# Inverse powers of one head pair and half of a decayed tile on GpSimd, row numbers at a later item, and loads of 96 rows in place of 128

## The chip, the cores and the metric

The kernel runs on one core of a Trainium2 chip. The metric is the device time of one execution in microseconds (us), taken as the median of several runs of the same program. Engine names are those of the profile: PE is TensorE (matmuls), PEld its weight loads, DVE is VectorE, ACT is ScalarE, POOL is GpSimd and SP is SyncE, which here only issues DMAs.

## The reference

Two blocks follow each other. The first is a linear recurrence over time (RWKV): 4 batches, 8 heads, 768 steps, head dimension 48.

```
for t in range(S):
    cur     = (u * k[t]) outer v[t]
    y[t]    = r[t] @ (state + cur)
    state   = w[:, None] * state + k[t] outer v[t]
```

The outputs are laid side by side as x (4 x 768 x 384) and go through a gated mixture of 8 experts: a token takes the expert with the largest logit, or, where a locality gate says so, the expert of the token before it; the result is p[e] * relu(x w1[e]) w2[e], with 1024 hidden units.

## The kernel before

**Items.** The attention is worked through in 16 items. Item n is batch n // 4 and head pair hp = n % 4; two heads of 48 rows lie in partitions 0 to 47 and 64 to 111, and the 16 rows behind each are zeros. The 768 steps are cut into 6 chunks of 128. Within a chunk the decay is taken out by scaling: r times powers of w (`rw`), k times inverse powers of w (`kw`), so that the chunk's inner part is an ordinary masked matmul; between chunks a state is carried.

**Per item, by engine.** POOL makes `pd` = r k (L217), `ke` = k times the powers up to the chunk's end (L213), and from item 3 on `rw` (L230, through `decayed`). DVE makes `kw` (L237), for items 0 to 2 also `rw` (L230), masks the scores into `am` (L293), multiplies `y` by v (L276) and scans the states `S` (L255). PE does the scores (L291, in two halves), the own term (L268), `added` (L249, k v products), `inside` (L300), `before` (L313) and the transposes of a finished item (L332). ACT copies results out of PSUM.

**Order.** The code's order is the order of each engine; `run` writes it out by hand. In iteration n an item's scores and own term are made, then `added`, `states`, and `scale(n + 1)`, which is POOL's work for the next item. `inside`, `before` follow in the next iteration. The early iterations 0, 1 and 2 have an order of their own.

**Powers of w.** `tab` in SBUF holds, for each head pair, powers 0 to 128 of w and of a reciprocal of w. `reciprocals(i)` refines the inverse powers by one Newton step: two DVE instructions (L156, L157) of which the second writes `inv[:, i]` into PSUM, where `kw` reads it. `self.first` is a copy in PSUM of the powers of the pair that is being worked on, made by ACT (L377, L392); it shares the bank `mp` with `T`, where `added` puts its sums. `reciprocals(0)` runs at the start, 1 in iteration 0, 2 in iteration 1 and 3 in iteration 3.

**Loads.** `load(n)` issues three DMAs on SP's queue: `rk` (r and k, 768 KB), `kv` (k and v by tokens, 584 KB) and `vT` (v transposed, 384 KB); `rk` of item 0 goes in two halves. Items 0 to 2 are loaded ahead of the loop, item n + 3 at the top of iteration n. `rk` and `vT` have `AHEAD` = 4 buffers, `kv` has 5, so that item n writes over item n - 4 (n - 5 for `kv`). SP's queue is worked through in order, and a DMA that waits for its buffer holds up those behind it.

**Router.** `numbering` makes nine tables of whole numbers with POOL's iota (L636), in iteration 2 ahead of `scale(3)`; `cast` has ACT turn six of them into floats in iteration 6 (L690). Their first reader is `experts_of(0, (0,))` in iteration 9. The experts' matmuls (L1134 and after) begin when the attention is done.

**Banks.** `banks` hands out two pairs of PSUM banks in turn; `warm(n)` takes the next pair and issues n transposes of the identity into it (L163), whose result is not used. In iteration 0 `warm(3)` stands between `turn_ends` (L173, L174: the turned powers of pairs 1 to 3, `endT`) and `added(0)`.

Of the kernel before, what the change touches and what calls it, by code (L numbers as in the profile page):

```python
# [11 lines left out]
F32 = mybir.dt.float32  # L12
I32 = mybir.dt.int32
Act = mybir.ActivationFunctionType
Alu = mybir.AluOpType
# [5 lines left out]
P = 128  # L21
B, H, S, DH = 4, 8, 768, 48
HP = H // 2
DP = 64
# [4 lines left out]
NCH = S // P  # L29
# [32 lines left out]
class Attention:  # L62
# [13 lines left out]
    def __init__(self, tc, st, rk_d, kv_d, vT_d, x_d, w_t, wp_d, kept, ident, lt, mp):  # L76
        self.tc, self.nc = tc, tc.nc
        nc = tc.nc
        self.rk_d, self.kv_d, self.vT_d, self.x_d = rk_d, kv_d, vT_d, x_d
        self.w_t, self.kept, self.ident, self.lt = w_t, kept, ident, lt  # L80

        self.late = st.enter_context(tc.tile_pool(name="late", bufs=1))
        self.wp = self.late.tile([P, H, 32], F32, name="wp")
        self.inner = ExitStack()

        def pool(name, bufs, **kw):
            return self.inner.enter_context(tc.tile_pool(name=name, bufs=bufs, **kw))

        once = pool("once", 1)
        self.two = pool("two", 2)  # L90
        self.four = pool("four", 4)
        self.py = pool("py", 1, space=PSUM)
        ps = pool("ps", 1, space=PSUM)

        self.pairs = [ps.tile([P, 2, 512], F32, name=f"pair{i}") for i in range(2)]

        self.T = mp[:, 2 * P + 2:2 * P + 2 + (NCH - 1) * DH].rearrange("p (e c) -> p e c", c=NCH - 1)

        self.inv = pool("pinv", 1, space=PSUM).tile([P, HP, P], F32, name="inv")


        n = B * HP - 1
        self.rks, self.vTs = [None] * AHEAD, [None] * AHEAD
        for i in range(1, AHEAD + 1):
            self.rks[(n + i) % AHEAD] = once.tile([P, 2, NCH, P], F32, name=f"rk{i}")
        for i in range(1, AHEAD + 1):
            self.vTs[(n + i) % AHEAD] = once.tile([P, 2, C2, P], F32, name=f"vT{i}")
        self.kvs = [once.tile([P, 2 * VB + DP - DH], F32, name=f"kv{i}") for i in range(AHEAD + 1)]
        self.items = [dict() for _ in range(B * HP)]
        self.xTs, self.xs, self.lTs = {}, {}, {}  # L110
        for i in range(AHEAD - 1):
            self.load(i)
        nc.sync.dma_start(out=self.wp, in_=wp_d)


        self.step = once.tile([P, HP, DH, NCH - 1], F32, name="step")
        nc.vector.memset(self.step, 0.0)


        self.tab = tab = once.tile([P, HP, 2, P + 1], F32, name="tab")  # L120
        nc.vector.memset(tab[:, 0, :, 0:1], 1.0)
        nc.gpsimd.memset(tab[:, 1:, :, 0:1], 1.0)
        w = once.tile([P, HP, 2], F32, name="w")
        nc.vector.tensor_scalar(w[:, :, 0], w_t[:, :, 0], W_LO, W_HI, Alu.max, Alu.min)
        nc.vector.reciprocal(w[:, :, 1], w[:, :, 0])
        nc.vector.tensor_copy(tab[:, 0, :, 1], w[:, 0])
        nc.gpsimd.tensor_copy(tab[:, 1:, :, 1], w[:, 1:])
        n = 2
        while n <= P:
            m = min(n - 1, P + 1 - n)  # L130
            for engine, t in ((nc.vector, tab[:, :1]), (nc.gpsimd, tab[:, 1:])):
                engine.tensor_mul(t[..., n:n + m], t[..., 1:1 + m], t[..., n - 1:n].to_broadcast([P, t.shape[1], 2, m]))
            n += m

        self.first, self.newton = mp[:, :P + 1], mp[:, P + 1:2 * P + 1]
        nc.scalar.copy(self.first, tab[:, 0, 0])
        self.reciprocals(0)

        self.end = once.tile([P, HP, P + DP], F32, name="end")
        self.endT = once.tile([P, 2, HP, 2 * DH], F32, name="endT")  # L140
        self.align(26)
        self.warm(8)
        self.ends(slice(0, 1))
        self.turn_ends(slice(0, 1))
        self.warm(5)
# [7 lines left out]
    def reciprocals(self, i):  # L153

        nc, inv = self.nc, self.tab[:, i, 1, 1:]
        nc.vector.scalar_tensor_tensor(self.newton, self.first[:, 1:], -1.0, inv, Alu.mult, Alu.mult)  # L156
        nc.vector.scalar_tensor_tensor(self.inv[:, i], self.newton, 2.0, inv, Alu.add, Alu.mult)  # L157

    def warm(self, n):

# [28 lines left out]
    def load(self, n):  # L189
        nc = self.nc  # L190
        b, hp = divmod(n, HP)
        rk, vT, kv = self.rks[n % AHEAD], self.vTs[n % AHEAD], self.kvs[n % (AHEAD + 1)]
        if n:
            nc.sync.dma_start(out=rk.rearrange("p a c t -> p (a c t)"), in_=self.rk_d[b, hp])
        else:
            for z in (slice(0, C2), slice(C2, NCH)):
                nc.sync.dma_start(out=rk[:, :, z], in_=self.rk_d[b, hp].rearrange("p (a c t) -> p a c t", a=2, c=NCH)[:, :, z])
        nc.sync.dma_start(out=kv, in_=self.kv_d[b, hp])
        nc.sync.dma_start(out=vT.rearrange("p a c t -> p (a c t)"), in_=self.vT_d[b, hp])
        self.items[n].update(b=b, hp=hp, rT=rk[:, 0], kT=rk[:, 1], vT=vT,  # L200
                             k=kv[:, :VB].rearrange("p (c x) -> p c x", c=NCH), v=kv[:, VB:])

    def scale(self, n):

        nc, t = self.nc, self.items[n]
        t["ke"] = self.two.tile([P, NCH, 2 * DH], F32, name="ke")
        t["pd"] = self.two.tile([P, NCH, P], F32, name="pd")
        t["rw"] = self.four.tile([P, NCH, P], F32, name="rw")
        hp = t["hp"]

        def ke(p):
            z = slice(p, NCH if n == 0 else NCH - 1, 2)
            nc.gpsimd.tensor_mul(t["ke"][:, z], t["k"][:, z], spread(self.endT[:, p, hp], 1, len(range(NCH)[z])))  # L213

        def pd(i):
            z = slice(i * C2, (i + 1) * C2)
            nc.gpsimd.tensor_mul(t["pd"][:, z], t["rT"][:, z], t["kT"][:, z])  # L217

        def rw(i):
            self.decayed(nc.gpsimd, n, slice(i * C2, (i + 1) * C2))  # L220


        for what in (pd, ke) if n < 3 else (ke, rw, pd) if n == 4 else (rw, ke, pd):
            for i in range(2):
                what(i)

    def decayed(self, engine, n, z):
        t = self.items[n]
        pw = self.first[:, :P] if n < 3 else self.tab[:, t["hp"], 0, :P]
        engine.tensor_mul(t["rw"][:, z], t["rT"][:, z], spread(pw, 1, z.stop - z.start))  # L230

    def keys(self, n):
        nc, t = self.nc, self.items[n]
        t["kw"] = self.two.tile([P, NCH, P], F32, name="kw")
        inv = self.inv[:, t["hp"]]
        for z in (slice(0, NCH),) if n > 2 else (slice(0, C2), slice(C2, NCH)):
            nc.vector.tensor_mul(t["kw"][:, z], t["kT"][:, z], spread(inv, 1, z.stop - z.start))  # L237
            if n < 3:
                self.decayed(nc.vector, n, z)

    def added(self, n):
# [113 lines left out]
    def run(self, router, fetch, heads):  # L355
# [11 lines left out]
        for n in range(M + 1):  # L367
            if n + AHEAD - 1 < M:
                self.load(n + AHEAD - 1)
            if n == 0:  # L370
                self.scale(0)
                self.keys(0)
                self.tables()
                self.scores(0, 0)()
                self.scores(0, 1)()
                self.own(0)
                self.nc.scalar.copy(self.first, self.tab[:, 1, 0])  # L377
                self.turn_ends(slice(1, HP))
                self.warm(3)
                self.added(0)  # L380
                self.reciprocals(1)
                self.states(0)
                self.scale(1)
                continue
            if n < 3:

                self.keys(n)
                self.inside(n - 1)
                self.before(n - 1)
                if n == 2:  # L390
                    self.turn(0, pair("tp"))
                self.nc.scalar.copy(self.first, self.tab[:, n + 1, 0])  # L392
                self.scores(n, 0)()
                keep = self.scores(n, 1)
                keep()
                self.own(n)
                self.added(n)
                self.states(n)
                if n == 1:
                    self.reciprocals(2)  # L400
                else:
                    router.numbering()
                self.scale(n + 1)
                continue
            if n < M:
# [19 lines left out]
                router.slots(0)  # L425
            if n == M:
                router.shares(0)
            if n + 1 < M:
                self.scale(n + 1)
            if n == g + 6:  # L430
# [9 lines left out]
                router.same(0, 1)  # L440
            if M - 2 <= n < M:
                fetch(2 * (n - M + 2) + 1)
            if n == 6:
                router.cast()
            if n == M:
                break
# [1331 lines left out]
```

## Time and profile before

| | us |
|---|---|
| median of 3 runs (lowest, highest) | 377.44 (376.11, 377.89) |
| the profiled execution, its own time | 379.17 |
| span from its first to its last instruction | 377.5 |
| PE busy in the span | 363.0 |
| DVE busy | 247.7 |
| POOL busy | 148.7 |
| ACT busy | 110.3 |
| first matmul of the experts (L1134) starts at | 113.02 |

Times in the text are counted from the span's first instruction. The attention is the first 113 us of it, the experts the rest. In the engines' timelines a row gives the start, the time that the group took, the engine, the line, the operation, the tiles written and read, and in brackets how long the engine had been idle and what ended that. A group joins instructions of one line that follow each other.

### The profile page before, as it was taken

How to read it: one execution, taken by the hardware profiler on the slowest of the kernel's cores; microseconds unless marked ns; L12 is line 12 of the kernel's file. 1: busy time of each engine (PE TensorE's matmuls, PEld its weight loads, DVE VectorE, ACT ScalarE, POOL GpSimd, SP SyncE). 2: the span in 40 equal slices, each digit the busy share in tenths (PEclk: the TensorE clock that was granted, in tenths of full speed). 3: DMA queues.
4: the chain of work that ended last, by engine and by line, in shares of the span. 5: the costliest groups of instructions: out<-in, count | busy, mean ns of one | idle time of the engine just before them, and what ended most of it. 6: DMA issues, size and time to landing. Idle time of an engine off the chain costs nothing. (4 is left out here: it accounts for less than half of the span.)

```text
span 377.5 us, 9676 instructions
## 1 busy us (share of the span) xinstructions
PE 363.0 (96%) x3844; PEld 319.6 (85%) x3844; DVE 247.7 (66%) x718; ACT 110.3 (29%) x304; POOL 148.7 (39%) x207
## 2 busy tenths in 40 slices
PE   7899999999989999999999999999999999999992
PEld 6676777786769998999899999999999998989971
DVE  6988778888834835787557656857767767555300
ACT  4132233233532211322332233333243233331210
POOL 7689999786222055212333113313233023021012
PEclk9999999999999999999999999999999999999998
DMA  7999999983669457713352452164165065162011
GB/s 245 417 411 410 407 405 338 370 300 109 196 232 340 160 188 296 299 27 115 140 198 62 147 214 87 49 218 190 38 207 213 22 215 206 21 257 112 2 41 38
DMA packets 17765, 74.93 MB, mean 199 GB/s; under 512 B 2778, under 2 KB 6624, under 8 KB 15408
## 3 DMA queue, kind: packets, MB, share of 16 engines
q1 hardware_dynamic: 10336, 56.89, 40.7%
q0 software_dynamic: 3424, 9.48, 7.4%
q10 hardware_dynamic: 3952, 7.87, 5.7%
q8 instruction: 32, 0.52, 0.6%
q14 instruction: 21, 0.17, 0.1%
HBM read 64.79 MB, written 9.47 MB: 197 GB/s over the span
## 5 line engine op out<-in xcount | busy, mean ns | idle before, releaser
L1333 POOL DMA_INDIRECT out_dram<-yo,sid x27 | 26.6, 985 | 115.5 <-ACT yo L1328 92.0
L1184 PE MATMUL h<-exT,w1t 128*128 128x168 f32 (+4 forms) x240 | 54.9, 327 | 0.0
L1188 DVE TENSOR_TENSOR hT<-h,hs 128x168 f32<-128x168 f32 (+3 forms) x60 | 21.1, 351 | 46.1 <-PE h L1184 29.6
L1107 POOL DMA_INDIRECT xg<-x_d,gid x29 | 31.1, 1072 | 34.1 <-DVE gid L877 15.1
L1184 PEld LDWEIGHTS h<-exT,w1t 128*128 128x128 f32 x240 | 41.6, 190 | 0.3 <-issue 0.3
L1134 PE MATMUL h<-exT,w1t 128*128 128x168 f32 (+2 forms) x192 | 37.2, 333 | 0.5 <-DVE lt L698 0.5
L1253 PE MATMUL y<-factors,sums 128*128 128x192 f32 x168 | 36.8, 326 | 0.0
L293 DVE TENSOR_TENSOR am<-pair,kept 128x768 f32<-128x768 f32 x32 | 30.0, 953 | 8.9 <-PE pair L291 8.4
L217 POOL TENSOR_TENSOR pd<-rk 128x384 f32<-128x384 f32 x32 | 31.5, 1006 | 10.6 <-PE y L268 10.0
L1184 PE MATMUL h<-xs,ws 128*128 128x168 f32 (+4 forms) x144 | 35.3, 327 | 0.0
L1134 PEld LDWEIGHTS h<-exT,w1t 128*128 128x128 f32 x192 | 30.9, 190 | 2.6 <-DVE lt L698 0.6
L1184 PEld LDWEIGHTS h<-xs,ws 128*128 128x128 f32 x144 | 25.5, 190 | 4.3 <-ACT hs L1191 1.2
L1253 PEld LDWEIGHTS y<-factors,sums 128*128 128x128 f32 x168 | 28.9, 190 | 0.2
L291 PE MATMUL pair<-rw,kw 48*64 48x128 f32 (+1 forms) x768 | 23.4, 249 | 1.9 <-issue 1.1
L300 PE MATMUL y<-am,kv 128*64 128x128 f32 x360 | 22.9, 276 | 1.3 <-DVE y L276 1.2
L230 POOL TENSOR_TENSOR rw<-rk,tab 128x384 f32<-128x384 f32 x26 | 23.7, 936 | 0.4 <-DMA rk<-in_rk_dram 0.4
L1121 DVE COPY exT<-tp 128x384 f32<-128x384 f32 (+5 forms) x29 | 13.9, 485 | 14.7 <-PE tp L1120 14.6
L291 PEld LDWEIGHTS pair<-rw,kw 48*64 48x64 f32 x768 | 19.6, 133 | 4.6 <-issue 2.8
L1253 PE MATMUL y<-w2t,hT 128*128 128x192 f32 x96 | 23.0, 328 | 0.0
L213 POOL TENSOR_TENSOR ke<-kv,endT 128x288 f32<-128x288 f32 (+1 forms) x32 | 21.9, 705 | 1.9 <-DMA kv<-in_kv_dram 1.0
L321 ACT COPY xT<-y 128x768 f32<-128x768 f32 x15 | 12.0, 800 | 33.1 <-PE y L313 31.1
L300 PEld LDWEIGHTS y<-am,kv 128*64 128x64 f32 x360 | 19.4, 137 | 2.4 <-DVE y L276 1.7
(298 smaller groups left out, 736.6 us busy)
## 6 DMA issues: line engine op xcount, KB each, us to landing
w1t<-in_w_dram SPq DMA_DIRECT2D x8, 1536.0 KB, 6.9
w2t<-in_w_dram SPq DMA_DIRECT2D x8, 1536.0 KB
rk<-in_rk_dram SPq DMA_DIRECT2D x15, 768.0 KB, 8.4
kv<-in_kv_dram SPq DMA_DIRECT2D x16, 584.0 KB, 7.1
vT<-in_vT_dram SPq DMA_DIRECT2D x16, 384.0 KB
x_d<-x ACTq DMA_DIRECT2D x4, 1152.0 KB
w1t<-in_w_dram SPq DMA_DIRECT2D x2, 768.0 KB
w2t<-in_w_dram SPq DMA_DIRECT2D x2, 768.0 KB
```

Of the source, the lines that this page charges most:

```text
L213: nc.gpsimd.tensor_mul(t["ke"][:, z], t["k"][:, z], spread(self.endT[:, p, hp], 1, len(range(NCH)[z])))
L217: nc.gpsimd.tensor_mul(t["pd"][:, z], t["rT"][:, z], t["kT"][:, z])
L230: engine.tensor_mul(t["rw"][:, z], t["rT"][:, z], spread(pw, 1, z.stop - z.start))
L291: nc.tensor.matmul(sc[f * DP:(f + 1) * DP, h, i, x:], lhsT=t["kw"][q, c, o * DP:(o + 1) * DP], rhs=t["rw"][q, c, x:], start=True, stop=True)
L293: return lambda: nc.vector.tensor_mul(t["am"][:, g], sc, spread(self.kept[:, g:g + 3], 1, 2))
L300: nc.tensor.matmul(t["y"][h][p * DP:(p + 1) * DP, c2 * P:(c2 + 1) * P], lhsT=t["v"][:, (2 * c + h) * DH:(2 * c + h) * DH + DP], rhs=t["am" ...
L1107: self.nc.gpsimd.indirect_dma_start(out=xg[:n], out_offset=None, in_=self.x_d[:rows], in_offset=bass.IndirectOffsetOnAxis(ap=u["gid"][:n, ...
L1134: nc.tensor.matmul(h[:, :n], lhsT=u["w1"][:, m, kk, :], rhs=u["xT"][:, kk, :], start=(kk == 0), stop=(kk == DK - 1))
L1184: nc.tensor.matmul(out, lhsT=a, rhs=b, start=start and k == 0, stop=stop and k == len(terms) - 1, skip_group_check=True)
L1188: nc.vector.tensor_tensor(out, a, b, op=Alu.add)
L1253: return lambda: nc.tensor.matmul(bank[:, x * half:(x + 1) * half], lhsT=a, rhs=b, start=(j == 0 and x == 0), stop=(j == FK // 2 - 1), ski ...
L1333: self.nc.gpsimd.indirect_dma_start(out=out.rearrange("n (h d) -> (n h) d", h=2) if half else out, out_offset=bass.IndirectOffsetOnAxis(ap ...
```

## The change

- `inverse(1)`, three POOL instructions into a new SBUF tile `more` and an ACT copy into `inv[:, 1]`, stands in the place of the two DVE instructions of `reciprocals(1)`. It comes behind `turn_ends` in iteration 0, and `warm(3)` there is gone.
- Of item 2's four `rw`/`kw` pieces on DVE, the second half of `rw` goes to POOL, as the first thing of `scale(2)`; POOL reads the powers from `tab` and not from `self.first`.
- `numbering` and `cast` go from iterations 2 and 6 to iteration 8.
- Items 4 to 15 load partitions 0 to 47 and 64 to 111 of `rk` and `vT`, each in two DMAs of 48 rows; the zeros in the other rows are those that items 0 to 3 left in the four buffers. `kv` stays whole. For item 4 `kv` is issued ahead of `rk`.

```diff
+        self.more = once.tile([P, P], F32, name="more")
...
+    def inverse(self, i):
+
+        nc, w, inv = self.nc, self.tab[:, i, 0, 1:], self.tab[:, i, 1, 1:]
+        nc.gpsimd.tensor_mul(self.more, w, inv)
+        nc.gpsimd.tensor_scalar(self.more, self.more, -1.0, 2.0, Alu.mult, Alu.add)
+        nc.gpsimd.tensor_mul(self.more, self.more, inv)
+        nc.scalar.copy(self.inv[:, i], self.more)
...
-        if n:
-            nc.sync.dma_start(out=rk.rearrange("p a c t -> p (a c t)"), in_=self.rk_d[b, hp])
-        else:
-            for z in (slice(0, C2), slice(C2, NCH)):
-                nc.sync.dma_start(out=rk[:, :, z], in_=self.rk_d[b, hp].rearrange("p (a c t) -> p a c t", a=2, c=NCH)[:, :, z])
-        nc.sync.dma_start(out=kv, in_=self.kv_d[b, hp])
-        nc.sync.dma_start(out=vT.rearrange("p a c t -> p (a c t)"), in_=self.vT_d[b, hp])
+        rows = (slice(0, P),) if n < AHEAD else (slice(0, DH), slice(DP, DP + DH))
+        src = self.rk_d[b, hp].rearrange("p (a c t) -> p a c t", a=2, c=NCH)
+        if n == AHEAD:
+            nc.sync.dma_start(out=kv, in_=self.kv_d[b, hp])
+        for z in (slice(0, NCH),) if n else (slice(0, C2), slice(C2, NCH)):
+            for q in rows:
+                nc.sync.dma_start(out=rk[q, :, z], in_=src[q, :, z])
+        if n != AHEAD:
+            nc.sync.dma_start(out=kv, in_=self.kv_d[b, hp])
+        for q in rows:
+            nc.sync.dma_start(out=vT[q].rearrange("p a c t -> p (a c t)"), in_=self.vT_d[b, hp][q])
...
+        if n == 2:
+            rw(1)
         for what in (pd, ke) if n < 3 else (ke, rw, pd) if n == 4 else (rw, ke, pd):
...
     def decayed(self, engine, n, z):
-        pw = self.first[:, :P] if n < 3 else self.tab[:, t["hp"], 0, :P]
+        pw = self.first[:, :P] if n < 3 and engine is self.nc.vector else self.tab[:, t["hp"], 0, :P]
...
     def keys(self, n):
-            if n < 3:
+            if n < 2 or n == 2 and z.start == 0:
                 self.decayed(nc.vector, n, z)
...
                 self.turn_ends(slice(1, HP))
-                self.warm(3)
+                self.inverse(1)
                 self.added(0)
-                self.reciprocals(1)
                 self.states(0)
...
                 if n == 1:
                     self.reciprocals(2)
-                else:
-                    router.numbering()
...
+            if n == HP * 2:
+                router.numbering()
             if n + 1 < M:
                 self.scale(n + 1)
...
-            if n == 6:
+            if n == HP * 2:
                 router.cast()
```

## The prediction

> **What bounds the kernel now.** The chain that ended last holds nothing here but the final scatter, so I read the stretches first (columns: PE, PEld, DVE, ACT, POOL busy with counts, granted clock, share of the DMA engines, GB/s).
>
> ```profile
> 28.00:45.00 17.00, 15.99 (x373) 11.57 (x362) 13.26 (x35) 3.50 (x8) 17.00 (x21) 1.00 1.02 410
> 45.00:104.00 59.00, 58.11 (x1270) 44.61 (x1270) 48.99 (x76) 20.16 (x53) 43.76 (x52) 1.00 0.80 291
> ```
>
> From 45 us on PE has no idle time worth the name; between 28 and 45 PE, POOL and the DMA engines are all nearly full, so the order of waiting must tell which one leads. The change's first two parts lie ahead of that, in items 0 to 2. There I read DVE's and PEld's timelines against each other.
>
> ```profile
> 10.64 0.96 DVE L276 TENSOR_TENSOR y<-y,vT 128x768 f32<-128x768 f32 x1
> 12.22 0.30 DVE L156 SCALAR_TENSOR_TENSOR mp<-mp,tab 128x128 f32<-128x128 f32 x1 [0.63 <-PE mp L249]
> ...
> 12.77 0.64 DVE L255 TENSOR_TENSOR_SCAN S<-step,mp 128x240 f32<-128x240 f32 x1
> 13.32 0.53 DVE L237 TENSOR_TENSOR kw<-rk,inv 128x384 f32<-128x384 f32 x1
> ...
> 14.70 0.55 DVE L230 TENSOR_TENSOR rw<-rk,mp 128x384 f32<-128x384 f32 x1
> 15.37 1.82 DVE L293 TENSOR_TENSOR am<-pair,kept 128x768 f32<-128x768 f32 x2
> 17.11 0.96 DVE L276 TENSOR_TENSOR y<-y,vT 128x768 f32<-128x768 f32 x1
> ...
> 21.99 1.89 DVE L293 TENSOR_TENSOR am<-pair,kept 128x768 f32<-128x768 f32 x2 [0.72 <-PE pair L291]
> ```
>
> ```profile
> 10.78 0.34 PEld L163 LDWEIGHTS pair<-ident 128*128 128x128 f32 x3
> 11.29 0.66 PEld L249 LDWEIGHTS mp<-kv,ke 128*64 128x64 f32 x20 [0.17 <-issue]
> 11.87 1.29 PEld L300 LDWEIGHTS y<-am,kv 128*64 128x64 f32 x24
> 13.46 0.68 PEld L313 LDWEIGHTS y<-rw,S 48*48 48x48 f32 x20 [0.30 <-DVE S L255]
> 14.43 0.57 PEld L291 LDWEIGHTS pair<-rw,kw 48*64 48x64 f32 x24 [0.29 <-issue]
> 15.30 0.54 PEld L291 LDWEIGHTS pair<-rw,kw 48*64 48x64 f32 x24 [0.30 <-DVE rw L230]
> ...
> 18.12 1.29 PEld L300 LDWEIGHTS y<-am,kv 128*64 128x64 f32 x24 [0.95 <-DVE y L276]
> 19.58 0.68 PEld L313 LDWEIGHTS y<-rw,S 48*48 48x48 f32 x20 [0.17 <-issue]
> 20.41 0.58 PEld L332 LDWEIGHTS pair<-ident,xT 112*128 112x128 f32 x6
> 21.14 0.54 PEld L291 LDWEIGHTS pair<-rw,kw 48*64 48x64 f32 x24
> ```
>
> In iteration 1 DVE leads: PE waits for `S`, for `rw`, then 0.95 us for `y`. In iteration 2 it is turned round: DVE has done `rw` and waits 0.72 us for PE's scores, which start when the transposes are through. So what DVE is spared in iteration 1 counts, and what it is spared in iteration 2 need not. POOL's rows and SP's (each SP issue here waits until the transfer eight issues before it has landed) give the third limit:
>
> ```profile
> 8.93 1.56 POOL L213 TENSOR_TENSOR ke<-kv,endT 128x288 f32<-128x288 f32 x2
> ...
> 13.88 1.36 POOL L213 TENSOR_TENSOR ke<-kv,endT 128x288 f32<-128x288 f32 x2 [1.03 <-DMA kv<-in_kv_dram]
> 16.77 1.96 POOL L217 TENSOR_TENSOR pd<-rk 128x384 f32<-128x384 f32 x2 [1.53 <-PE y L268]
> ...
> 20.00 0.15 POOL L636 IOTA ie_i<- 128x8 int32 x1
> ...
> 20.83 0.13 POOL L636 IOTA ief_i<- 1x8 int32 x1
> 21.37 1.69 POOL L230 TENSOR_TENSOR rw<-rk,tab 128x384 f32<-128x384 f32 x2 [0.42 <-DMA rk<-in_rk_dram]
> ...
> 27.19 1.35 POOL L213 TENSOR_TENSOR ke<-kv,endT 128x288 f32<-128x288 f32 x2 [0.89 <-PE y L313]
> ...
> 56.22 1.97 POOL L217 TENSOR_TENSOR pd<-rk 128x384 f32<-128x384 f32 x2 [0.55 <-PE y L268]
> ```
>
> ```profile
> 21.36 0.33 SPq L199 DMA_DIRECT2D vT<-in_vT_dram  x1
> 22.81 0.33 SPq L194 DMA_DIRECT2D rk<-in_rk_dram  x1
> 23.77 0.33 SPq L198 DMA_DIRECT2D kv<-in_kv_dram  x1
> ...
> 27.10 0.33 SPq L194 DMA_DIRECT2D rk<-in_rk_dram  x1
> ```
>
> Eight issues back, these four stand for the landings of `rk`, `kv`, `vT` of item 3 and `kv` of item 4. POOL's starts at 21.37 and 27.19 are thus landings (the profile names PE at 27.19, but the matmul that frees that buffer was long done; the `pd` at 16.77 I take for `rk` of item 2 in the same way). Loads hold POOL up until 27.19 and not after.
>
> **The change, part by part.**
>
> *`warm(3)` gone.* Three transposes, 0.34 us of weight loads, and the 0.17 us idle behind them: `added(0)` can begin at about 10.85 and not 11.29, 0.44 us sooner; its `ke` was done at 8.93 + 1.56 = 10.49. `inside(0)` gains less, since it needs `y`: 10.64 + 0.96 = 11.60, and 0.05 us on (as at 18.12, behind 17.11 + 0.96) is 11.65 in place of 11.87. As heaters the transposes are not missed: PE waits longer, 0.95 us, at 18.12, and the granted clock after it is 1.00. The pairs of banks change places from here on; the only one in use, that of `endT`, is read by 11.71 (below): 0.
>
> *`reciprocals(1)` gone from DVE.* L156 waited for `added(0)` to end; now the scan stands there, at 12.22 - 0.44 = 11.78 in place of 12.77, and `kw`, `rw` follow 0.99 us sooner: the first `kw` at 12.33, the last `rw` done at 14.70 + 0.55 - 0.99 = 14.26. PE takes over as the limit: L313 starts 1.46 us behind L300 (19.58 - 18.12), at 13.11; the scores 0.83 us after that (20.41 - 19.58), at 13.94, with the first half's `rw` there, and the second half's before it is wanted; `am` 0.85 us on (21.99 - 21.14), at 14.79, against 15.37. **Gain 0.58 us.** `y` of item 1 moves by the same, 17.11 to 16.53.
>
> *`inverse(1)` on POOL and ACT.* The nearest rows, with mean ns of one after the bar:
>
> ```profile
> L132 POOL TENSOR_TENSOR tab<-tab 128x192 f32<-128x192 f32 x1 | 0.5, 512 | 0.1
> L132 POOL TENSOR_TENSOR tab<-tab 128x96 f32<-128x96 f32 x1 | 0.4, 352 | 0.1
> masks.py:199 POOL TENSOR_SCALAR_AFFINE_SELECT ident<-ident 128x128 f32<-128x128 f32 x1 | 0.3, 284 | 0.0
> L230 POOL TENSOR_TENSOR rw<-rk,tab 128x384 f32<-128x384 f32 x4 | 3.7, 934 | 0.4 <-DMA rk<-in_rk_dram 0.4
> ```
>
> A product 128 wide is 352 + 32 x 1.67 = 405 ns; the scalar step, not seen on POOL, lies between 284 and 405, I take 350; with the 0.1 us of idle time that the L132 rows show between dependent steps the three are 1.35 us: 10.49 to 11.85. Bounds: three times 284 (0.85 us) and three times 934, for steps three times as wide (2.8 us, and 0.2 between them: done at 13.5). Then ACT copies 128 columns, behind this:
>
> ```profile
> 11.07 0.64 ACT L174 COPY endT<-pair 128x576 f32<-128x576 f32 x1 [2.05 <-PE pair L173]
> ```
>
> That row (576 columns in 0.64 us) ends at 11.71 and does not delay it; at 0.3 us for the copy `inv` is there at 12.15, 0.2 us before `kw` wants it. At the upper bound it is there at 13.8, `kw` comes 0.5 us later than before, and the gain of 0.58 becomes a loss of 0.5. Behind `inverse` on POOL waits `pd` of item 1, some 1.97 us long: done at 13.8, which the load of `kv` covers (13.88); `ke` keeps its time.
>
> *Half of item 2's `rw` on POOL.* DVE is spared 0.46 us (the step between starts), ahead of an `am` that has 0.72 us to spare: gain 0. POOL does 0.93 us at 16.77, then `pd` and `ke` (1.96 and 1.36) until 21.0. The iotas, nine in 0.96 us from 20.00 to 20.96, are no longer there; `rw` of item 3 starts at 21.37 as before, since its load has not moved. So removing `numbering` here buys nothing and pays for the added piece. With that cover gone `rw` of item 3 would end after 23.06, and PE wants it only behind item 2's `am` and `y`, 21.99 + 1.89 + 0.96 = 24.8.
>
> *`numbering` in iteration 8.* 0.95 us on POOL ahead of item 9's `rw`, `ke` and `pd`. The last of these waits 0.55 us for PE anyway (56.22), and the first is wanted by the scores here:
>
> ```profile
> 59.28 1.27 PE L291 MATMUL pair<-rw,kw 48*64 48x128 f32 x46
> ```
>
> Cost 0. The six small casts go to an ACT that is busy 20.16 of 59 us: 0.
>
> *Loads of 96 rows.* Per item 288 KB less, five DMAs in place of three. `kv` of item 3 (584 KB) took 22.81 - 21.36 = 1.45 us and `vT` (384 KB) 0.96 us: 411 GB/s both, back to back. Item 4's `kv`, now first, lands at 23.77 + 1.45 = 25.2 and not 27.10, the halves of `rk` (288 KB, 0.72 us each) by 26.7. POOL's `ke` then starts when `pd` of item 3 ends (27.19 - 0.89 = 26.30), 0.9 us sooner. But PE waits for POOL nowhere in that stretch; POOL works ahead and has to wait for PE at 56.22. Gain 0, and the two further issues of SP per item (0.33 us each) lie in SP's waits. The readers of `rk` and `vT` wait for two transfers each, which have both landed: 0. [...]
>
> Sum: -0.58 us, kept to the end because every later step hangs on PE. Against the profiled execution 379.17 becomes 378.6 and its span 376.9; against the median, which lies 1.7 below that execution, 377.44 becomes **376.9**.
>
> **The rivals.**
>
> *DVE pays in full* (0.15). If PE's steps in items 1 and 2 can be drawn in, DVE's 0.99 + 0.46 = 1.45 us counts: 376.0. For it: DVE's rows show no idle time between 12.22 and 21.99 but the 0.72 us; against it those 0.72 us, which PE ends.
>
> *The gain is used up* (0.16). `inverse` is near its upper bound: 377.2 to 377.9. For it: the scalar step is not seen on POOL.
>
> *Loads bound it* (0.04). 12 x 288 KB at 411 GB/s are 8.6 us: 368.8. For it the share of 1.02 until 45 us; against it POOL's wait for PE, not for a load, at 56.22.
>
> *Slower: loads starve* (0.04). Eight transfers in flight were 2.7 items and are 1.6. Here is how long one took, and the pace of the items:
>
> ```profile
> DMA to landing us min/median/max: 5.8/7.1/11.7
> L276 DVE TENSOR_TENSOR y<-y,vT x15: 956/966/967, 10.6 to 99.9; 128x768 f32<-128x768 f32 x15
> ```
>
> The items' mean pace is (99.9 - 10.6) / 14 = 6.4 us. It decides once a transfer takes over 8 x 6.4 / 5 = 10.2 us; at 11.7 an item comes every 7.3 us, 11 items lose up to 10 us: 387. Against it: that time is queueing, and 1.6 items of 1.48 MB at 411 GB/s are 5.8 us.
>
> *Slower: POOL stops at a kind of instruction it has not run yet* (0.03). Three us or more at 10.5 delay `kw`; 5 us put its end at 15.5, ACT's copy behind it, and `kw` at 15.9 in place of 13.32: 380. Against it: the first iota, at 20.00, follows without idle time. [...]
>
> **How the numbers follow.** The forecast (a gain of 0.2 to 0.9 us) has 0.58, and with it 376.9 is likeliest. The runs before spread from 376.11 to 377.89, so about 0.5% is what can be told from no change; 0.5% faster is below 375.6, slower above 379.3. The range takes in 1.45 us of gain and the loss of 0.5, with some of the runs' spread, 375.7 to 378.4, and leaves out the three rare cases. Faster: the loads' case and a tail of the full gain, 0.09; slower: the two starving cases and a tail, 0.07.
>
> **What would show it.** `am` of item 1 starts near 14.8 and `y` near 16.5, with `kw` waiting for no ACT; `rw` of item 3 on POOL still at 21.3 to 21.4; `ke` of item 4 near 26.3; `am` of item 2 again behind PE; the experts' first matmul 0.6 us before 113.02. A wait of POOL or PE for `rk`, `kv` or `vT` after 30 us, or a `kw` behind ACT, proves it wrong.

## The result, and the profile after

The changed kernel takes 396.55 us (median of 6 runs, 392.68 to 400.11) beside 377.65 us for the kernel before (6 runs, 376.11 to 378.84). Two of its six runs, the profiled one among them, are slow ones, over 1.5% above the fastest, and are left out of the ratio: 1.046, 95% interval 1.040 to 1.052. It is 17 to 19 us slower; the forecast was 376.9 us and no change that can be told.

The profiled execution took 400.11 us, with a span of 398.4 us. The experts' first matmul, at 113.02 us before, stands here (PE's timeline of the changed kernel: start, us, line, tiles):

```profile
132.21 3.26 PE L1148 MATMUL h<-exT,w1t 128*128 128x168 f32 x12 [0.50 <-DVE lt L712]
```

So 19.2 us are lost in the attention; from there to the end of the span it is 266.2 us, 264.5 before. The same stretches as before (PE, PEld, DVE, ACT, POOL busy with counts, granted clock, DMA share, GB/s):

```profile
28.00:45.00 17.00, 14.98 (x268) 10.61 (x268) 10.82 (x13) 2.68 (x6) 12.13 (x14) 0.80 1.03 220
45.00:104.00 59.00, 50.27 (x1018) 37.70 (x1019) 37.02 (x73) 12.93 (x32) 41.19 (x57) 0.93 0.92 236
```

The DMA engines are as full as they were (1.03 and 1.02) and move 220 GB/s in place of 410. The trace keeps every packet of a transfer, and a row of `rk` is one packet of 6144 bytes: in this stretch its median time was 0.24 us before (494 packets) and 0.45 us after (269). A full share is thus no proof of speed: an engine also counts as busy while its packet is slow. PE did 268 matmuls where it did 373, at a clock of 0.80. POOL waits for these loads. Its groups on the page before, and then after (count, busy, mean ns, then the idle time ahead of the group and what ended most of it):

```profile
L230 POOL TENSOR_TENSOR rw<-rk,tab 128x384 f32<-128x384 f32 x26 | 23.7, 936 | 0.4 <-DMA rk<-in_rk_dram 0.4
...
L213 POOL TENSOR_TENSOR ke<-kv,endT 128x288 f32<-128x288 f32 (+1 forms) x32 | 21.9, 705 | 1.9 <-DMA kv<-in_kv_dram 1.0
```

```profile
L245 POOL TENSOR_TENSOR rw<-rk,tab 128x384 f32<-128x384 f32 x27 | 24.5, 929 | 13.1 <-DMA rk<-in_rk_dram 11.6
...
L226 POOL TENSOR_TENSOR ke<-kv,endT 128x288 f32<-128x288 f32 (+1 forms) x32 | 21.8, 705 | 14.7 <-DMA kv<-in_kv_dram 11.2
```

The list of waits from 24 to 133 us has (us in total, times, longest):

```profile
POOL ke L226 <- DMA kv<-in_kv_dram: 10.5, 7, 4.6
...
POOL rw L245 <- DMA rk<-in_rk_dram: 9.8, 7, 4.2
```

That is 20.3 us. From 24 to 113 us of the kernel before, the list names no wait of POOL for a load (the 0.89 us at 27.19 us, which it gives to PE, the prediction took for one). The sum is near the 19.2 us that are lost, but it does not explain them: in the same list PE's matmuls wait for POOL nowhere, for DVE 0.8 us, and 10.8 us stand under "issue".

PE, the engine that was full, shows where the time goes. From 8 us to the experts' first matmul it was busy 100.9 of 105.0 us before, at a mean clock of 1.00; now it is busy 110.1 of 124.2 us, at 0.92. That is 10.0 us more of idle time and 9.2 us more of work at a lower clock, together the 19.2 us. Of the idle time 10.9 us lie in five stops (PE's timeline, the rows behind them):

```profile
29.68 1.41 PE L306 MATMUL pair<-rw,kw 48*64 48x128 f32 x39 [2.65 <-issue]
...
58.20 0.80 PE L264 MATMUL mp<-kv,ke 128*48 128x48 f32 x14 [2.63 <-issue]
...
72.91 0.83 PE L360 MATMUL pair<-xT,wp 128*32 128x384 f32 x2 [2.22 <-issue]
...
81.21 1.28 PE L283 MATMUL y<-pd,w_t 48*64 48x384 f32 x5 [1.63 <-issue]
...
102.01 1.55 PE L283 MATMUL y<-pd,w_t 48*64 48x384 f32 x7 [1.73 <-issue]
```

Each stop is in the middle of a line's matmuls, and "issue" means that the profile names nothing that PE waits for. One of the DMA queues on the page is called `instruction` (32 packets in the span, 0.52 MB, so 16 KB each):

```profile
q8 instruction: 32, 0.52, 0.5%
```

Each of the five stops ends 1.4 to 1.7 us after one of these packets did. The kernel with the loads alone, which comes below, also has five stops of 1.6 us or more up to its experts' first matmul, after the same numbers of weight loads and matmuls of PE (948, 1957, 2464, 2717 and 3477 recorded ones; the steps between them are multiples of about 253), each ending 1.35 to 1.6 us after such a packet. In other kernels of this study some of the stops come at these numbers too, and in the kernel before the one at 3477 alone, 0.84 us long. I read this as PE waiting for its own instructions, late with the loads as those of the queue `instruction` would be. It is read from places and times, and not shown; no wait names it and no run takes that queue away.

The lower clock follows the stops: by the trace's record it was 0.50 for 6.8 us from 30.3, for 3.4 us from 57.6 and from 81.5, and for 6.8 us from 102.0, while the 24 matmuls of `inside` at 34.45 us took 2.79 us in place of 1.53. I take it for a consequence; no run separates it.

The early items went as worked out, and a little better. DVE and POOL there (the item's `S`, `kw`, `am`, `y`; then the three steps of `inverse`, and the first late `ke`):

```profile
11.45 0.65 DVE L270 TENSOR_TENSOR_SCAN S<-step,mp 128x240 f32<-128x240 f32 x1 [0.27 <-PE mp L264]
12.02 0.53 DVE L252 TENSOR_TENSOR kw<-rk,inv 128x384 f32<-128x384 f32 x1
...
14.10 1.82 DVE L308 TENSOR_TENSOR am<-pair,kept 128x768 f32<-128x768 f32 x2
15.84 0.96 DVE L291 TENSOR_TENSOR y<-y,vT 128x768 f32<-128x768 f32 x1
...
20.71 2.06 DVE L308 TENSOR_TENSOR am<-pair,kept 128x768 f32<-128x768 f32 x2 [1.11 <-PE pair L306]
```

```profile
10.02 0.42 POOL L163 TENSOR_TENSOR more<-tab 128x128 f32<-128x128 f32 x1
10.54 0.29 POOL L164 TENSOR_SCALAR more<-more 128x128 f32<-128x128 f32 x1
10.92 0.46 POOL L165 TENSOR_TENSOR more<-more,tab 128x128 f32<-128x128 f32 x1
11.33 1.97 POOL L230 TENSOR_TENSOR pd<-rk 128x384 f32<-128x384 f32 x2
...
21.42 1.69 POOL L245 TENSOR_TENSOR rw<-rk,tab 128x384 f32<-128x384 f32 x2 [0.38 <-DMA rk<-in_rk_dram]
...
28.83 1.34 POOL L226 TENSOR_TENSOR ke<-kv,endT 128x288 f32<-128x288 f32 x2 [2.49 <-DMA kv<-in_kv_dram]
...
65.36 1.68 POOL L245 TENSOR_TENSOR rw<-rk,tab 128x384 f32<-128x384 f32 x2 [4.18 <-DMA rk<-in_rk_dram]
```

Up to 21.42 us everything is on time. The `ke` of item 4, the first with loads of 96 rows, starts at 28.83 us where 26.3 was forecast, though its own `kv` is a whole transfer and was issued first. In the packets of that `kv` (4672 bytes each) the reason can be seen: those that started before 22.7 us took 0.18 to 0.20 us, and the last 25, from 22.8 us on and beside the first half transfers, 0.26 to 0.62 us.

### The profile page after: what moved, and what is told of

Read it like the earlier page. It is cut to its first block, busy times and chain, and to the rows that moved or that the text cites. A ratio compares the mean times of both kernels' runs of the same rounds, so it can differ in the third digit from the quotient of the medians.

```text
span 398.4 us, 9725 instructions
## 1 busy us (share of the span) xinstructions
PE 374.4 (94%) x3841; PEld 327.2 (82%) x3841; DVE 247.1 (62%) x715; ACT 110.2 (28%) x305; POOL 150.5 (38%) x211
## 5 line engine op out<-in xcount | busy, mean ns | idle before, releaser
L1198 PEld LDWEIGHTS h<-exT,w1t 128*128 128x128 f32 x240 | 41.6, 190 | 0.3 <-issue 0.3
L1148 PE MATMUL h<-exT,w1t 128*128 128x168 f32 (+2 forms) x192 | 38.5, 341 | 0.5 <-DVE lt L712 0.5
L1148 PEld LDWEIGHTS h<-exT,w1t 128*128 128x128 f32 x192 | 32.0, 196 | 2.7 <-DVE lt L712 0.6
L245 POOL TENSOR_TENSOR rw<-rk,tab 128x384 f32<-128x384 f32 x27 | 24.5, 929 | 13.1 <-DMA rk<-in_rk_dram 11.6
L226 POOL TENSOR_TENSOR ke<-kv,endT 128x288 f32<-128x288 f32 (+1 forms) x32 | 21.8, 705 | 14.7 <-DMA kv<-in_kv_dram 11.2
L315 PE MATMUL y<-am,kv 128*64 128x128 f32 x360 | 25.5, 296 | 0.8 <-DVE y L291 0.8
L315 PEld LDWEIGHTS y<-am,kv 128*64 128x64 f32 x360 | 22.0, 150 | 1.8 <-DVE y L291 1.1
## 6 DMA issues: line engine op xcount, KB each, us to landing
rk<-in_rk_dram SPq DMA_DIRECT2D x24, 288.0 KB, 10.2
```

Of the source, the lines that this page charges most:

```text
L315: nc.tensor.matmul(t["y"][h][p * DP:(p + 1) * DP, c2 * P:(c2 + 1) * P], lhsT=t["v"][:, (2 * c + h) * DH:(2 * c + h) * DH + DP], rhs=t["am" ...
L1148: nc.tensor.matmul(h[:, :n], lhsT=u["w1"][:, m, kk, :], rhs=u["xT"][:, kk, :], start=(kk == 0), stop=(kk == DK - 1))
L1198: nc.tensor.matmul(out, lhsT=a, rhs=b, start=start and k == 0, stop=stop and k == len(terms) - 1, skip_group_check=True)
```

## Which part of the change it is

**The changed kernel with the loads of before** (`load` as it was, the rest changed):

> The changed kernel with the loads of before (128 rows, three transfers per item): GpSimd's inverse powers, the moved half of r, the moved row numbers and the missing warm-up stay. Theory (the loads alone lost the time): the loads move at 410 GB/s again, no clock loss, 376.6 to 377.0, that is 0.5 to 1 us below the kernel before. Rival (POOL's added work or the missing warm-up share in the loss): 380 or more.

Measured: 378.29 us, ratio 0.9988 (0.9968 to 1.0008): the loss is gone, and the gain of 0.5 to 1 us that was expected is not there either. Its stretch from 28 to 45 us and the experts' first matmul:

```profile
28.00:45.00 17.00, 15.90 (x363) 11.78 (x366) 12.57 (x34) 3.48 (x7) 17.00 (x22) 1.00 1.02 410
```

```profile
112.51 1.98 PE L1144 MATMUL h<-exT,w1t 128*128 128x168 f32 x12 [0.49 <-DVE lt L708]
```

**The kernel before with the loads of 96 rows alone:**

```diff
+ rows = (slice(0, P),) if n < AHEAD else (slice(0, DH), slice(DP, DP + DH))
  ...
+         for q in rows:
+             nc.sync.dma_start(out=rk[q, :, z], in_=src[q, :, z])
```

> The kernel before with nothing but the loads of 96 rows. Theory: all of the loss, 394 to 399, with 205 to 300 GB/s between 25 and 104 us at full DMA share. Rival (the other edits share in it): well below, 385 or less.

Measured: 395.71 us, ratio 1.042 (1.037 to 1.048), experts' first matmul at 131.05 us.

```profile
28.00:45.00 17.00, 15.33 (x275) 11.12 (x277) 11.14 (x14) 2.68 (x6) 12.12 (x14) 0.80 1.03 212
```

Within the noise the loads are all of the loss (1.042 and 1.046, with intervals that overlap), and the other edits none of it. The next runs ask why fewer bytes take longer.

## Not the number, not the 48 rows, not the rows left out

**As many transfers, cut by columns.** Every transfer has all 128 rows, and an item still has five:

```diff
+ for x in range(2):
+     nc.sync.dma_start(out=rk[:, x], in_=src[:, x])
```

> The kernel before; items 4 to 15 load rk and vT in two transfers each, split by columns, so that each keeps all 128 rows; all bytes are loaded, five transfers per item, kv of item 4 first. Theory A (the rows that a transfer reaches set its speed): 400 to 415 GB/s as before; the eight places in flight fill up sooner, so the store of x may hold SP up for a few us, hidden by the lead of the loads: 377 to 380. Rival B (five transfers in place of three, with eight in flight): the loss is there, 390 or more.

Measured: 380.09 us, ratio 1.0036 (1.0008 to 1.0063). Five transfers cost at most 2.4 us (0.0063 of 378.45), so rival B falls. In its profile, of an execution with TensorE's clock at 0.65 throughout, the loads still moved 403 GB/s from 18 to 28 us and 368 from 28 to 45.

**Halves of 64 rows, all bytes:** `slice(0, DP), slice(DP, P)`, partitions 0 to 63 and 64 to 127, in place of the 48 rows, for `rk` and `vT` of items 4 to 15, two thirds of an item's bytes.

> [...] Theory A (half of the partitions is half of the speed): about 205 GB/s for these two thirds of the bytes, slower than with 48 rows: 402 to 425. [...] Rival B (number of transfers): as with the columns cut in two.

Measured: 405.09 us, ratio 1.070 (1.066 to 1.075).

```profile
28.00:45.00 17.00, 14.34 (x251) 10.17 (x252) 10.38 (x13) 2.68 (x6) 10.61 (x13) 0.80 1.03 221
```

Half a partition range runs at about half the rate of 410 GB/s whether it is 48 rows (212) or 64 (221), and more bytes take longer, 405.09 us for 395.71. The median packet of `rk` took 0.43 us. Theory A of these texts, half of the partitions for half of the speed, agrees as far as this row goes. The cause that it names, half of the paths, is an assumption of mine that no run shows. A forbids the next result.

**One transfer of 112 rows**, `(slice(0, U),)`, which reaches both halves:

> Kernel before, with rk and vT of items 4 to 15 loaded as one transfer each of rows 0 to 111 (112 of 128; the 16 rows left out are not read). Bytes of an item 672 + 584 + 336 = 1592 KB for 1744 (-8.7%). Theory A (a transfer whose rows lie in one half of the partitions has half of the paths, so a transfer lasts as long as its fuller half needs): the fuller half still has 64 rows, so each transfer lasts as long as one of 128 rows; 28 to 45 us shows about 410 x 1592/1744 = 374 GB/s at a full DMA share, time 377.5 to 379, no gain. Rival D (the rate goes by the rows of a transfer, whichever they are: 48 rows 212 GB/s, 64 rows 221, 128 rows 410, so 112 rows about 365): the same rate, so this run does not tell A from D. Rival E (any transfer that isn't all 128 partitions is slow): 220 to 240 GB/s in 28 to 45 us, 388 us or more. Rival F (bytes alone at 410 GB/s): 405 to 410 GB/s, transfers shorter, 376.5 to 378.5.

Measured: 397.21 us, ratio 1.054 (1.048 to 1.060).

```profile
28.00:45.00 17.00, 12.78 (x253) 8.89 (x252) 10.82 (x13) 2.68 (x6) 13.11 (x17) 0.90 1.02 245
```

Only 12.5% of the rows are missing, in one transfer as before, and the rate is 245 and not the 374 GB/s that A needs. A as it stands falls; so does D, which wanted 365. (The texts count a whole item as 1744 KB; 768 + 584 + 384 are 1736, and A's 374 becomes 376.) The median packet of `rk` took 0.41 us, nearly as long as in halves, and the DMA share is 1.02: all engines are at work, each packet is slow.

**The halves on two queues**, the upper one issued by ACT:

```diff
+ (nc.scalar if q.start else nc.sync).dma_start(out=rk[q, :, z], in_=src[q, :, z])
```

> Kernel before, with the loads of 96 rows, where the lower 48 rows of rk and vT are issued by SP as in the changed kernel and the upper 48 rows by ACT, on ACT's own queue. Theory A (each half reaches half of the paths): with both halves in flight at once the paths are all used again, so 28 to 45 us shows 350 GB/s or more (212 with both on one queue), the clock there is back near 1.0, and the time falls from 395.7 to 378 to 386, what is left over 378.5 being ACT held up by the waits for free buffers that now stand in its own order. Rival D (a transfer of 48 rows has half the rate whatever else is in flight): 212 to 235 GB/s, 391 us or more.

Measured: 404.73 us, ratio 1.068 (1.060 to 1.075).

```profile
28.00:45.00 17.00, 14.96 (x279) 10.86 (x272) 11.05 (x16) 2.90 (x6) 12.06 (x15) 0.81 1.03 197
```

From 28 to 33 us packets of both queues are under way, at 190 GB/s; from 34 to 40 us ACT's queue has none, and the rate is 208. Halves in flight together are no faster: the second blow to A in its simple form. That the time is 9 us above that of one queue fits ACT's list of waits, where copies out of PSUM now stand behind issues that wait for a free buffer or a landed transfer (one of 9.2 us for `rk`); this was not followed up.

**The stores of x.** In the changed kernel two issues of SP wait 10.1 and 8.7 us for a store of x to land, which I read as stores and loads sharing the eight places. The stores of the first three batches were given to POOL:

```diff
- nc.scalar.dma_start(out=self.x_d[b * S:(b + 1) * S, :].rearrange("(c p) d -> p c d", p=P), in_=x)
+ self.stores.append((b, x))        # issued by nc.gpsimd after before(n - 1)
```

> Kernel before, with the loads of 96 rows as in the changed kernel, and the x stores of the first three batches issued by POOL a little later than by ACT now (the last one stays with ACT). It takes away the two waits of SP for an x store (10.1 and 8.7 us in the changed kernel). Theory A1 (the half rate of the loads is all of the loss): those waits go but the loads are still late, 28 to 45 us as before this edit (212 GB/s), time 392 to 396. Rival A2 (half rate is half of it, the loads held behind the stores the rest): 382 to 390, and the first experts' matmul at least 6 us before the 131.05 of the kernel with the loads alone.

Measured: 396.62 us, ratio 1.052 (1.047 to 1.056). The two waits are gone from SP's list and the time has not moved (395.71 with them), with the experts' first matmul at 129.51 us, only 1.5 us before 131.05: they were a symptom.

**Only `vT` in halves:**

> Kernel before, with vT alone of items 4 to 15 as two transfers of 48 rows, rk as one of 128 (a third of the halves' bytes: 288 of 864 KB an item). Theory A with the queue as the limit: an item's transfers need 768 KB at 410 GB/s 1.92 + 584 KB 1.46 + 288 KB at 160 to 212 GB/s 1.4 to 1.8 = 4.8 to 5.2 us, under the 6.1 us of an item (1744 KB at 291 GB/s from 45 to 104 us), so the loads keep up once they have caught up: 377.5 to 380.5, and 28 to 45 us at 310 to 350 GB/s with a full DMA share. Rival (loss in proportion to the halves' bytes): 378.5 + 17.3/3 = 384.

Measured: 387.28 us, ratio 1.025 (1.019 to 1.031).

```profile
28.00:45.00 17.00, 14.56 (x291) 10.09 (x285) 12.07 (x31) 2.68 (x6) 16.54 (x20) 0.90 1.03 301
```

A third of the halves' bytes costs half of the loss, 9.2 of 17.3 us. Both expectations missed, 377.5 to 380.5 and 384. The rate, 301, is just below the expected 310 to 350. At 301 GB/s the 1640 KB of an item would take 5.6 us, an estimate that is still under the 6.1 us of the expectation, so it is the step from rate to time that was too simple. PE shows it: up to the experts' first matmul at 121.80 us it is idle 5.4 us longer than before and works 3.4 us longer, at a mean clock of 0.97.

## Where the rows lie

What 48, 64 and 112 rows have in common is that they are not 128. The next kernels take the same number of rows in other places. Theory G, as they put it to the test, is an assumption of mine: a transfer of rows 32 to 95 goes at the full rate, one of rows 0 to 31, 0 to 63, 64 to 95, 64 to 127 or 96 to 127 at half of it. Why the place should count is in no trace here. G's numbers are estimates from these two rates, with the 414 GB/s that the kernel before moved from 23 to 28 us as the full one, and from the bytes of an item; for 48 and 112 rows it has none. A would say the same of rows 32 to 95, since they lie in both halves, but A has failed at 112 rows, with 374 for 245. The rival E: whatever isn't 128 rows is slow.

**Rows 32 to 95 and 0 to 31**, against **0 to 63 and 64 to 95**. Rows 96 to 127 are not read, so tokens are routed otherwise and the program leaves its fast path for the experts (2768.22 and 2776.51 us in all); only the attention is read in these two.

> Kernel before, with rk and vT of items 4 to 15 as two transfers each, of rows 32 to 95 and of rows 0 to 31 (rows 96 to 127 are not read). Same rows, bytes and number of transfers as the next kernel; only the cut differs. [...] Rival E (any transfer that isn't all 128 rows is slow): 210 to 260 GB/s and 388 us or more.

> As the kernel with rows 32 to 95 and 0 to 31, but cut into rows 0 to 63 and 64 to 95 (the same rows and bytes). [...] Rival E: the same as its pair, within 2 us.

Measured, the first kernel and then the second:

```profile
28.00:45.00 17.00, 14.93 (x291) 11.11 (x293) 12.03 (x34) 2.68 (x6) 16.34 (x19) 0.91 1.01 278
```

```profile
28.00:45.00 17.00, 14.26 (x251) 10.08 (x252) 10.61 (x13) 2.68 (x6) 12.12 (x15) 0.80 1.04 219
```

The experts' first matmul comes at 119.33 and 129.47 us: 10.1 us between two kernels with the same rows, bytes and number of transfers. Of these, 5.8 us are idle time of PE and 4.3 us the lower clock (table below). E falls. G's sizes are too good, 346 for 278 and 260 for 219, and both rates miss the ranges that I had set, 330 to 350 and 235 to 260.

**The same with every row loaded**, so that the whole time counts: rows 32 to 95, 0 to 31, 96 to 127, against 0 to 63, 64 to 95, 96 to 127.

> Kernel before, with rk and vT of items 4 to 15 as three transfers each, rows 32 to 95, 0 to 31 and 96 to 127: all rows and bytes are loaded. Its pair has the same bytes and the same seven transfers an item, with the cut at 64 in place of 32. [...] Rival E (any transfer of fewer than 128 rows is slow, wherever its rows lie): as its pair, 400 us or more.

> As the kernel with rows 32 to 95, 0 to 31 and 96 to 127, cut into rows 0 to 63, 64 to 95 and 96 to 127. Theory G: all three at half rate, 7.14 us an item as in the kernel with two transfers of 64 rows (405.1 us, 221 GB/s): 401 to 409 us, 28 to 45 us at 205 to 230 GB/s, and at least 8 us slower than its pair. Rival E: within 2 us of its pair.

Measured: 398.31 us (ratio 1.048, 1.043 to 1.054) and 407.11 us (1.074, 1.069 to 1.080), 8.8 us between them; the intervals are apart. The sizes again miss: the first is 1.3 us above my estimate of 388 to 397 us, and from 28 to 45 us both show nearly one rate, 242 and 241 GB/s, the second above its range of 205 to 230. They part later:

```profile
45.00:104.00 59.00, 49.70 (x1022) 38.45 (x1019) 35.49 (x71) 12.83 (x32) 36.97 (x44) 0.91 0.89 263
```

```profile
45.00:104.00 59.00, 46.24 (x883) 34.63 (x871) 30.10 (x48) 11.74 (x31) 33.86 (x40) 0.86 0.92 240
```

Up to the experts' first matmul PE is idle 19.3 and 19.9 us in the two; what parts their times there, 133.12 and 138.02 us, is the lower clock of the second. So this pair bears out the rates from 45 us on, and less than its times seem to say.

**Source or destination?** So far the rows of DRAM moved with those of SBUF. What the rate goes by is "the meeting place" in the two texts, and G has it on the side of SBUF. One kernel takes the destination rows of the cut at 32 and the source rows of the cut at 64, the other the reverse (one execution each, 2768.13 and 2769.77 us in all; only the attention is read):

```diff
- nc.sync.dma_start(out=rk[q, :, z], in_=src[q, :, z])
+ nc.sync.dma_start(out=rk[q, :, z], in_=src[r, :, z])    # q: SBUF rows, r: DRAM rows
```

> As the kernel cut into rows 32 to 95 and 0 to 31, but the data come from DRAM rows 0 to 63 and 64 to 95: the destination rows of the one kernel of the pair with the source rows of the other. The values are other ones than the reference needs, so the experts take another path and only the attention is read (experts' first matmul 119.33 with the cut at 32, 129.47 with the cut at 64; 278 and 219 GB/s from 28 to 45 us). Theory G (the meeting place is on the side of SBUF): as with the cut at 32, 118 to 122.5 us and 260 to 295 GB/s. Rival H (it is on the side of DRAM): as with the cut at 64, 126 us or more and 205 to 235 GB/s.

> The other way round: destination rows 0 to 63 and 64 to 95, from DRAM rows 32 to 95 and 0 to 31. Theory G: 126 us or more, 205 to 235 GB/s. Rival H: 118 to 122.5 us, 260 to 295 GB/s.

Measured, the stretch from 28 to 45 us of each:

```profile
28.00:45.00 17.00, 16.03 (x369) 11.72 (x369) 12.77 (x35) 3.48 (x7) 15.64 (x19) 1.00 1.01 272
```

```profile
28.00:45.00 17.00, 13.73 (x297) 10.00 (x301) 11.92 (x34) 2.68 (x6) 12.94 (x17) 1.00 1.02 233
```

The rates go with the destination: 272 beside 278, and 233 beside 219. The time does so in the first (119.81 us to the experts' first matmul) and not in the second: 121.53 where 126 or more was expected. The clock accounts for that: it was 1.00 there up to the experts' first matmul and 0.93 in the kernel with the same destination rows, while PE's idle time is nearly the same in both, 13.0 and 13.5 us. The packets agree. From 28 to 45 us, of the packets of `rk` 161 of 302 took under 0.35 us with the cut at 32 and 132 of 281 with only its destination rows; with the cut at 64 it was none of 257, and 11 of 243 with only its destination rows. So the place that matters is on the side of SBUF, as far as one execution of each shows it.

**Rows 32 to 95 alone**, one transfer each for `rk` and `vT` (one execution, 2762.85 us in all; only the attention is read):

> rk and vT of items 4 to 15 as one transfer each, of rows 32 to 95 alone (the other 64 rows are not read, and the experts take another path). It asks whether that cut runs at full rate: 1160 KB an item. Theory G: 2.87 us an item, far under the pace of 6.1, so the loads catch up early, 18 to 28 us still shows 390 to 412 GB/s at a full DMA share, and the experts' first matmul is at 112 to 113.1 us, as in the kernel before (113.02). If rows 32 to 95 run at less than full rate as well (the pair's 278 GB/s for 346 worked out): 300 to 360 GB/s in 18 to 28 us.

Measured, with the experts' first matmul:

```profile
23.00:28.00 5.00, 4.92 (x124) 4.28 (x128) 4.20 (x8) 1.50 (x3) 5.00 (x7) 1.00 1.02 411
28.00:45.00 17.00, 16.31 (x361) 11.65 (x355) 13.36 (x36) 3.48 (x7) 16.46 (x21) 1.00 0.83 292
```

```profile
110.79 1.98 PE L1138 MATMUL h<-exT,w1t 128*128 128x168 f32 x12 [0.50 <-DVE lt L702]
```

411 GB/s with a full share, from 23 to 28 us, when only these transfers and whole `kv` are under way: a transfer of 64 rows can run at the rate of one of 128, and the median packet of `rk` is back at 0.24 us. With 64 rows from row 0 the rate was 221. From 28 us on the engines are no longer full, 0.83. This is the clearest row of the study. Loading less at full rate seems to pay, more than expected (112 to 113.1): 110.79 for 113.02 us with a third of the bytes gone. Counted from the first scores (7.44 and 7.86 us) that is 1.8 us.

| loads of items 4 to 15 (`rk`, `vT`) | GB/s, 28 to 45 us | estimate by G | experts' first matmul, us | PE idle, busy from 8 us to there, us | time, us |
|---|---|---|---|---|---|
| 128 rows (before) | 410 | 414 | 113.02 | 4.2, 100.9 | 377.44 |
| 32-95 alone | 411 (23 to 28 us) | 414 | 110.79 | 3.4, 99.4 | |
| `vT` alone in 48 + 48 | 301 | | 121.80 | 9.5, 104.3 | 387.28 |
| 32-95, 0-31 | 278 | 346 | 119.33 | 7.7, 103.7 | |
| 0-111 | 245 | | 129.92 | 14.2, 107.7 | 397.21 |
| 32-95, 0-31, 96-127 | 242 | 311 | 133.12 | 19.3, 105.8 | 398.31 |
| 0-63, 64-95, 96-127 | 241 | 249 | 138.02 | 19.9, 110.2 | 407.11 |
| 0-63, 64-127 | 221 | 249 | 136.40 | 19.6, 108.8 | 405.09 |
| 0-63, 64-95 | 219 | 260 | 129.47 | 13.5, 108.0 | |
| 48 + 48 (the change's loads) | 212 | | 131.05 | 12.7, 110.4 | 395.71 |

Read the rates for what a transfer does and the times for what that costs; the times hold the clock as well, and no run keeps it fixed. G is too high wherever a cut has a number: by 1% for rows 32 to 95 alone, by 3 and 13% for two cuts at 64, and by 19 to 29% in three, the cuts at 32 into several transfers and 0-63, 64-95. What is shown: at the same rows, bytes and number of transfers the rate changes with where the cut lies (278 and 219), and 64 rows can go at 411 or at 221. Why the place counts is not shown: which engine writes which row is in no trace here. Why 112 rows went at 245 GB/s and the misses in size stay open.

**The other edits once more**, in more rounds:

> The changed kernel with the loads of the kernel before (128 rows) once more, in more rounds: all that is left of the change is the inverse of pair 1 on POOL, half of item 2's decayed r on POOL, and the row numbers in item 8. Theory: experts' first matmul 0.5 us sooner as in its first profile (112.51 for 113.02): ratio 0.9975 to 0.9995, 377.0 to 378. Rival: no gain at all, ratio 1.000 within 0.001.

Measured: 378.67 us, ratio 1.0011 (0.9986 to 1.0036). With the first run's 0.9988 there is no gain to be told, and no version here beats the kernel before. The experts' first matmul is at 112.76 us in its profile.

## Why the prediction was wrong

**The step that failed** is "Loads of 96 rows", in its sentence that the halves of `rk` take 0.72 us each: it gives halves the rate of whole transfers. The rows it drew on, `kv` and `vT` at 411 GB/s, are transfers of different sizes and the same 128 partitions. They bear on the size, and nothing in them bears on fewer partitions; no lower bound was set for that, which the prediction did for other unseen prices. The runs put 212 GB/s in the place of 411 for the mix of halves and whole `kv`. "Gain 0" rested on POOL working ahead of PE. POOL lost that lead (20.3 us of waits), but what stopped PE was in the main something that the prediction has no term for: five stops of 10.9 us in all, which I read as late instructions, and a lower clock worth 9.2 us behind them.

**The rival "loads starve"** named the right place and the sign. Its condition, over 10.2 us from issue to landing, was just reached by `rk`. The page after has these medians (8.4 us for `rk` and 7.1 for `kv` before):

```profile
kv<-in_kv_dram SPq DMA_DIRECT2D x16, 584.0 KB, 8.5
rk<-in_rk_dram SPq DMA_DIRECT2D x24, 288.0 KB, 10.2
...
vT<-in_vT_dram SPq DMA_DIRECT2D x24, 144.0 KB, 9.5
```

It was put at 0.04 because of "1.6 items of 1.48 MB at 411 GB/s are 5.8 us", the same number again: at 212 GB/s they are 11.2 us. And it gave the fault to the number of transfers in flight, which the kernel cut by columns shows to cost 2.4 us at most.

**"Gain 0" for loading less**, apart from the rate, was perhaps too low as well: about 2 us at full rate, in one execution and with more rows left out. There POOL's `ke` of item 4 starts at 25.73 us without a wait; whether that is what led on to the end of the attention is not shown. The rival "loads bound it", with 8.6 us, was too high.

**Right:** `inverse` took 1.36 us (10.02 to 11.38) for 1.35, and its scalar step 0.29 us for an estimate of 0.35; POOL did not stop at the new kind of instruction: the scalar step began 0.10 us after the product ended, and the next product 0.09 us after that step. The 3 and 5 us of the rival "POOL stops" are suppositions, and no run shows such a stop. `am` of item 1 came 6.65 us after the first scores (14.10 - 7.45) for 7.51 before (15.37 - 7.86): 0.86 us sooner where 0.58 was worked out. Most of the difference is one step: the scores began 0.52 us behind the first of `before` (12.70 to 13.22), and the prediction had taken 0.83 from iteration 2. `am` of item 2 waited for PE, 1.11 us, and `rw` of item 3 started at 21.42 for 21.37. `numbering` cost POOL 0.95 us in item 8 with nobody waiting in the changed kernel, where it lies ahead of a wait of 4.18 us; with the loads of before it lies ahead of `rw` at 54.17 us, without idle time, and POOL waits 2.33 us for PE by 69.52. **What the gain became:** with the loads of before, POOL's `ke` of item 4 starts at 27.40 us, after 0.88 us for `kv`; it was 27.19. In the profile of that kernel's second run it is 26.61. In these two and in the kernel before it comes 5.82 or 5.83 us behind `rw` of item 3 (21.58, 20.78 and 21.37 us), which itself starts when its load has landed. The loads, at 410 GB/s without a pause, come at their own pace, and what the early items won is waited away there. The prediction had kept it "to the end because every later step hangs on PE".

## What to carry to other kernels

A rate read from transfers of all 128 partitions is shown for such transfers alone: before rows are cut from a load, time the cut shape, or keep the zeros and one whole transfer. Look at GB/s beside the DMA share: 410 and 212 GB/s came with shares of 1.02 and 1.03. When loads are slow, look at what the busiest engine itself waits for, and not only at who waits for the loads. And where a bound rests on one number, ask which row would change if that number were half.

## What was not expected of the hardware

- 64 rows from row 32 run at 411 GB/s, 64 rows from row 0 at 221; 112 of 128 rows at 245.
- A whole transfer among halves is slowed with them: `kv` of item 4, issued first, held POOL 2.49 us.
- Two queues do not mend it (197 GB/s).
- PE stopped five times in the changed kernel, 1.6 to 2.7 us each, in the middle of a line, and went on 1.4 to 1.7 us after a packet of the queue `instruction`.
